# Chunk 0's x by selection matrices, sums of channels two heads at a time, and a new order of the first third of the tasks, in a kernel of a recurrence and an MLP

## The chip, the core and the metric

The kernel runs on one core of a Trainium2 chip. The metric is the device time of one execution in microseconds. A core has five engines that run their own instruction queues side by side and meet at semaphores: TensorE (PE) for matmuls, VectorE (DVE), ScalarE (ACT), GpSimd (POOL) and SyncE (SP), which here issues the DMA transfers. All data are in float32.

## What is computed

For each batch and head a state of 40 x 40 is carried over 768 steps, read by r and updated with w, a, b, k and v. The outputs y of the 8 heads of a token stand side by side as a row x of 320 values, which goes through an MLP with a quick GELU.

```python
batch, n_heads, seq, head_dim = (4, 8, 768, 40)
for t in range(S):
    y[:, :, t] = np.einsum('bhd,bhde->bhe', rt, state)
    Sa = np.einsum('bhde,bhe->bhd', state, at)
    state_decay = state * wt[:, :, None, :] - np.einsum('bhd,bhe->bhde', Sa, bt)
    state = state_decay + np.einsum('bhd,bhe->bhde', vt, kt)
x = np.ascontiguousarray(attn_out.transpose(0, 2, 1, 3)).reshape(B * S, H * D)
h = x @ w_in                                # 320 x 2048
g = h * (1.0 / (1.0 + np.exp(-1.702 * h)))
return (g @ w_out).astype(np.float32)       # 2048 x 320
```

## The kernel before

The sequence is cut in 12 chunks of 64 steps, and the four batches in two pairs. A chunk of one pair is a unit; there are 24, and unit i belongs to chunk i // 2. Inside a unit the recurrence is turned into matrix work on 64 x 64 blocks, in these steps (names are those of the tiles):

- `load_w`, `logarithm`, `decay`: the decays w are loaded (`logw`), their logarithm is taken on ScalarE, and they are summed over time on PE with the triangular matrix `edges`. `by_time` writes the sums of all channels side by side (`ps_cum`). For units 0 to 3 `by_channel` writes the same sums with the channels on partitions (`ps_cumc`), one head to each of the four 64 x 64 quarters of PE, 16 matmuls per unit; later units get those by two scans on VectorE from a second tile `wc`. Exponentials of the sums are FT, GT and G.
- `prep`: a, k, b and the tiles `kh`, `bh` are multiplied by FT, GT or G, and the scores A and RV are made.
- `inverse`: the product N of a and b goes through five levels of an iteration for a triangular inverse. For units 0 to 3 (`plain_level`) a level is 16 matmuls with EX and PT and four with `ident` into `ps_level`, a copy of PT on ScalarE (or VectorE), and a transpose to EX on VectorE. After the last level Q, Tc, QT and T21 complete T.
- `solve`: B, then X = T B on PE, M on VectorE, then `read` writes `ps_y`. Its left part is y, its right part the next state (`zraw`, `zr`, `zT`, `rz` in the next unit of the pair). `decayed` multiplies y by FT to x, which lies with 40 channels on each half of the partitions.
- `part_with` writes x to DRAM in two transfers and `get_back` reads it in two (one for each half of the partitions) as `xT_all`, with 64 partitions of five rows of 128 tokens, so that a matmul contracts 64 of the 320 channels. `w_in` is laid out on the host in the same order of channels (`order`).
- `mlp`: per chunk `up` (160 matmuls of 64 x 64 x 256, four at a time), GELU, and `down` (128 matmuls of 64 x 64 x 320). `weight` turns the MLP weights, which come as 64-bit numbers in eight pieces of four transfers, into float32: one step on ScalarE (`rebased`), three on VectorE (`bounded`, `shifted`, `rounded`) and one on GpSimd (`joined`) for each piece.

The order of all this is written out by hand: `ORDER` is a text of task numbers, each with a letter for the engine, and `listed` turns it into the program. A digit behind p, a, d or g names the pair of PSUM banks; behind s it is the number of transfers that may be under way before the next one starts. Tasks are numbered as `plan.add` is called; the costs given there were for the planner that made the text, and the kernel does not use them. All matmuls but the new ones go through `mm` (L301), all transfers through `transfer` (L331), so the profile shows those lines for them.

## Time and profile before

| | us |
|---|---|
| median of 3 runs | 681.54 (681.05 to 681.87) |
| the profiled execution | 679.49 |
| its span, first to last instruction | 677.7 |
| PE busy | 649.6 |
| VectorE busy | 449.7 |
| ScalarE busy | 329.1 |
| GpSimd busy | 175.7 |

In a row of a group, "out<-in" names the tiles, "x" the number of instructions; behind the bar stand the busy time in us and the mean of one in ns, then the idle time ahead of them and what ended it. In a row of the timeline stand the start, the length, the engine, the line and the tiles. A float32 matmul of the program is two MATMUL records in the trace, so the counts there are twice those of the code. TensorE's matmuls overlap: the start of the next group, not the end of the last matmul, tells how long a group held the engine.

### The profile page before, as it was taken

How to read it: one execution, taken by the hardware profiler on the slowest of the kernel's cores; microseconds unless marked ns; L12 is line 12 of the kernel's file. 1: busy time of each engine (PE TensorE's matmuls, PEld its weight loads, DVE VectorE, ACT ScalarE, POOL GpSimd, SP SyncE). 2: the span in 40 equal slices, each digit the busy share in tenths (PEclk: the TensorE clock that was granted, in tenths of full speed). 3: DMA queues.
4: the chain of work that ended last, by engine and by line, in shares of the span. 5: the costliest groups of instructions: out<-in, count | busy, mean ns of one | idle time of the engine just before them, and what ended most of it. 6: DMA issues, size and time to landing. Idle time of an engine off the chain costs nothing.

```text
span 677.7 us, 42447 instructions
## 1 busy us (share of the span) xinstructions
PE 649.6 (96%) x19616; PEld 568.7 (84%) x19616; DVE 449.7 (66%) x916; ACT 329.1 (49%) x681; POOL 175.7 (26%) x201
## 2 busy tenths in 40 slices
PE   5777999999999999999999999999999999999997
PEld 4667787787999997888888899999889798799896
DVE  5777779777867668757776687868656766675001
ACT  3676745634564655654545445455344454263010
POOL 6541443324123123123113211322411421300000
PEclk9979999999999999999999999999999999999999
DMA  6875753415324314432404513513412411200200
GB/s 208 295 255 160 226 172 97 129 42 152 107 64 131 94 58 124 114 107 65 124 14 131 149 35 108 155 33 107 140 38 62 130 53 45 69 15 14 60 13 21
DMA packets 35473, 69.74 MB, mean 103 GB/s; under 512 B 5472, under 2 KB 14816, under 8 KB 35296
## 3 DMA queue, kind: packets, MB, share of 16 engines
q1 hardware_dynamic: 35216, 66.99, 32.9%
q8 instruction: 154, 2.52, 1.6%
q14 instruction: 23, 0.19, 0.1%
q10 hardware_dynamic: 80, 0.04, 0.0%
HBM read 59.15 MB, written 7.86 MB: 99 GB/s over the span
## 4 chain that ended last, share of the span: by engine, by line
PE 88%; DMA 6%; DVE 2%; issue 1%; SPq 1%; ACT 1%; DVEq 0%; ACTq 0%
PE ps_up L301 31%; PE ps_down L301 29%; PE ps_level L301 8%; PE ps_y L301 5%; PE ps_B L301 4%; PE ps_X L301 2%; PE ps_N L301 2%; PE ps_rz L301 1%; PE ps_RV L301 1%; PE ps_A L301 1%; PE ps_zT L301 1%; SPq L331 1%; DMA w_sb<-in_w_in 1%; PE ps_cum L301 1%; PE ps_T L301 1%
## 5 line engine op out<-in xcount | busy, mean ns | idle before, releaser
L301 PE MATMUL ps_up<-xT_all,w_sb 64*64 64x256 f32 x3840 | 253.3, 377 | 2.1 <-issue 1.3
L301 PE MATMUL ps_down<-w_sb,g 64*64 64x320 f32 (+1 forms) x3200 | 241.5, 419 | 0.2 <-ACT zr L879 0.2
L301 PEld LDWEIGHTS ps_up<-xT_all,w_sb 64*64 64x64 f32 x3840 | 170.8, 133 | 18.8 <-issue 2.1
L301 PEld LDWEIGHTS ps_down<-w_sb,g 64*64 64x64 f32 x3200 | 142.5, 133 | 31.6 <-issue 0.4
L1000 ACT ACTIVATE g<-ps_up 128x1024 f32<-128x1024 f32 x48 | 49.2, 1025 | 46.3 <-PE ps_up L301 45.8
L719 POOL TENSOR_TENSOR EX<-ES,quads 128x512 f32<-128x512 f32 x30 | 39.7, 1324 | 116.4 <-DVE ES L712 77.7
L761 ACT COPY W<-ps_level 128x512 f32<-128x512 f32 x56 | 32.8, 585 | 67.7 <-PE ps_level L301 66.0
L301 PEld LDWEIGHTS ps_level<-W,EX 64*64 64x64 f32 x2560 | 60.0, 134 | 5.4 <-DVE T L840 0.2
L763 DVE TENSOR_TENSOR E<-two,ps_level 128x256 f32<-128x256 f32 x80 | 33.1, 415 | 36.5 <-ACT W L761 32.3
L301 PE MATMUL ps_level<-W,EX 64*64 64x64 f32 (+1 forms) x2560 | 56.8, 217 | 0.0
L717 ACT ACTIVATE EX<-ES,quads 128x256 f32<-128x256 f32 x82 | 37.2, 501 | 31.9 <-DVE ES L712 31.3
L629 POOL TENSOR_TENSOR ak<-ak,FT 128x512 f32<-128x512 f32 x17 | 23.0, 1353 | 77.2 <-DMA ak<-in_ak 54.4
L301 PEld LDWEIGHTS ps_level<-PT,EX 64*64 64x64 f32 x1280 | 30.7, 138 | 11.5 <-DVE EX L733 3.3
L301 PE MATMUL ps_level<-PT,EX 64*64 64x64 f32 (+2 forms) x1280 | 32.5, 234 | 6.9 <-DVE EX L733 5.0
L712 DVE STREAM_TRANSPOSE ES<-E 128x256 f32<-128x256 f32 x80 | 35.3, 443 | 4.4
L301 PE MATMUL ps_y<-RV,kh 64*64 64x104 f32 (+1 forms) x768 | 35.4, 247 | 0.9 <-DVE M L917 0.9
L301 PE MATMUL ps_y<-M,bh 64*64 64x104 f32 (+1 forms) x768 | 35.5, 247 | 0.7 <-DVE M L917 0.5
L901 ACT COPY B<-ps_B 128x416 f32<-128x416 f32 (+1 forms) x35 | 17.2, 493 | 34.4 <-PE ps_B L301 34.2
L301 PEld LDWEIGHTS ps_y<-RV,kh 64*64 64x64 f32 x768 | 29.6, 133 | 3.2 <-DVE M L917 1.5
L917 DVE TENSOR_TENSOR M<-ps_X,later 128x832 f32<-128x832 f32 (+1 forms) x24 | 23.9, 995 | 10.2 <-PE ps_X L301 10.0
L301 PE MATMUL ps_B<-RV,A 64*64 64x104 f32 (+1 forms) x768 | 29.2, 252 | 0.8 <-issue 0.8
L637 POOL TENSOR_TENSOR kh<-time,G 128x320 f32<-128x320 f32 x18 | 16.2, 901 | 51.2 <-PE ps_y L301 34.6
(133 smaller groups left out, 1099.0 us busy)
## 6 DMA issues: line engine op xcount, KB each, us to landing
ak<-in_ak SPq DMA_DIRECT2D x48, 160.0 KB
rv<-in_rv SPq DMA_DIRECT2D x48, 160.0 KB
time<-in_time SPq DMA_DIRECT2D x24, 320.0 KB
xT_all<-x_dram SPq DMA_DIRECT2D x48, 160.0 KB
wc<-in_wc SPq DMA_DIRECT2D x20, 264.0 KB
logw<-in_w SPq DMA_DIRECT2D x24, 160.0 KB
RV<-in_v SPq DMA_DIRECT2D x24, 160.0 KB
b<-in_b SPq DMA_DIRECT2D x48, 80.0 KB
```

What stands on the lines that cost most here:

```text
L301: nc.tensor.matmul(o, lhsT, rhs, start=start, stop=True, skip_group_check=True)
L331: begun.append(queue.dma_start(dst, src).ins)
L629: plan.add(R, {"DVE": 690.0, "POOL": 1270.0, "sbuf": True}, lambda t: of(t.engine).tensor_mul(ahT(), ahT(), FT_of(i)), reads=T("ak", "FT") ...
L637: plan.add(R + 4, {"POOL": 870.0, "DVE": 490.0, "sbuf": True}, lambda t, n=n, dst=dst: of(t.engine).tensor_mul(dst(i)[:, :, :D], by_head(t ...
L712: plan.add(rank, dve(256), lambda t: nc.vector.transpose(ES(n), source(t)), writes=[key("ES", n, 6)], **reads)
L717: nc.scalar.activation(dst[:, :, h], ES(n), ACT.Copy, scale=quads[:, h, :1])
L719: of(t.engine).tensor_mul(dst, ES(n).unsqueeze(2).to_broadcast([128, 8, 2, 32]), quads.unsqueeze(1).to_broadcast([128, 8, 2, 32]))
L761: plan.add(rank, any2(512), lambda t: copy(t.engine)(tiles_of(W(n + 1)), blocks(psum(t, ""), 64)), writes=[key("W", n + 1, 5)], pair=pair)
L763: plan.add(rank, dve(256), lambda t: nc.vector.tensor_sub(tiles_of(E(n + 1)), every(two32, [128, 2, 4, 32]), blocks(psum(t, ""), 64)[:, :, ...
L901: plan.add(R, any2(4 * wide), lambda t: copy(t.engine)(dst(), some(psum(t, "")[:, :, :208])), writes=[("Bv", i)] if x and c > 0 else T("B" ...
L917: plan.add(R + 1, dve(8 * wide), lambda t: nc.vector.tensor_tensor(M_of(i)[:, :, :wide].rearrange("p (j b) n -> p b j n", b=2), some(psum( ...
L1000: plan.add(-45, {"ACT": 1030.0, "table": "gelu"}, lambda t: nc.scalar.activation(g_of(c * NQ + q).rearrange("p m r n -> p r m n"), psum(t, ...
```

## The change

There are four parts.

1. Chunk 0 (units 0 and 1) no longer goes through DRAM. `first_x` multiplies y by FT in two VectorE instructions instead of four. `chosen` then moves the channels to their partitions with five matmuls per unit against selection matrices of zeros and ones, one with 512 columns and four with 128, and one copy brings the result from PSUM to `xT_all`. `selections` builds the two matrices once, in six instructions at the start.
2. The order of channels in x, and with it that of the rows of `w_in`, is another one. For chunks 1 to 11 `get_back` therefore reads each unit by four transfers: for each half of the partitions one of four rows and one of the fifth.
3. Units 0 to 3 load w as `in_apart`, with each head's 40 channels padded to 64 by ones, into the tile `wc` (256 KB instead of 160). `by_channel` then takes two heads in one matmul over 128 columns of weights, 8 matmuls per unit instead of 16. The padded columns of `logw`, and the three instructions that cleared them, are gone.
4. `ORDER` is new in its first third. On PE the two programs are the same from the 254th group of equal matmuls on, out of 953; in it and on the other engines the work of the first units stands in another order: the first load is w of unit 0, then `time`, a and k, a quarter of a weight piece, and b; N of unit 0 stands ahead of A and RV; and the first `up` matmul stands behind level 4 of unit 2 and A of unit 3 in both, and behind RV of unit 3 in the old order alone.

```diff
-    logw_t = several("logw", [128, DM + 24])
-    for t in logw_t:
-        nc.gpsimd.memset(t[:, DM:], 0.0)
+    logw_t = several("logw", [128, DM])
...
-    logw_of = lambda i: logw_t[i % 3][:, :DM]
+    logw_of = lambda i: logw_t[i % 3] if i >= BY_PE else apart(i).rearrange("p (h d) -> p h d", h=H)[:, :, :D]
 
     wc_of = lambda i: buf("wc", i, [128, 2, 8 * 33])
+    apart = lambda i: wc_of(i).rearrange("p n h -> p (n h)")[:, :H * 64]
 
     def load_w(i):
-        for name, of, src, n in (("wc", wc_of, wc_d, 528), ("logw", logw_of, w_d, DM))[i < BY_PE:]:
+        for name, of, src, n in (("wc", wc_of, wc_d, 528), ("logw", logw_of, w_d, DM)) if i >= BY_PE else (("wc", apart, apart_d, H * 64),):
...
-            ps, lw = psum(t, "ps_cum"), logw_of(i)
+            ps, lw = psum(t, "ps_cum"), logw_of(i) if i < BY_PE else logw_of(i).rearrange("p (h d) -> p h d", h=H)
             for n in (1, 0):
                 for b in BITS:
                     u = b ^ n
-                    mm(ps[HALF[u], b, :160], incl[HALF[b]], lw[HALF[b], n * 160:(n + 1) * 160], True)
-        plan.add(R, pe((1, 160)), by_time, reads=T("log"), uses=T("logw"), room=T("G"), writes=T("cum"), pair=("cum", i))
+                    mm(ps[HALF[u], b, :160].rearrange("p (h d) -> p h d", d=D), incl[HALF[b]], lw[HALF[b], 4 * n:4 * n + 4], True)
+        plan.add(R, pe((1, 160)), by_time, reads=T("log"), uses=T("logw") if i >= BY_PE else T("wc"), room=T("G"), writes=T("cum"), pair=("cum", i))
 
         def by_channel(t):
 
             ps = psum(t, "ps_cumc")
             for u, f in product(BITS, BITS):
-                for b, e in QUARTERS:
-                    o, h = (2 * u + f) * 65, head(e, f, b, u) * D
-                    mm(ps[HALF[e], b, o:o + 65], logw_t[i % 3][HALF[b], h:h + 64], edges[HALF[b]], o == 0)
+                for b in BITS:
+                    o, h = (2 * u + f) * 65, head(0, f, b, u)
+                    mm(ps[:, b, o:o + 65], apart(i)[HALF[b], 64 * h:64 * h + 128], edges[HALF[b]], o == 0)
...
-                y = both(i)[:, at, :64] if c > 0 else part(t)[:, u, 2 * b:2 * b + 2, :64]
-                of(t.engine).tensor_mul(x[:, b ^ u, b], y, FT_of(i)[:, at])
-        if c > 0:
-            plan.add(R + 6, {"DVE": 1200.0, "POOL": 2300.0, "sbuf": True}, decayed, reads=T("y", "FT"), uses=T("rz"), writes=T("x"))
-        else:
-            plan.add(R + 6, {"DVE": 1000.0}, decayed, reads=T("FT"), writes=T("x"), pair=("y", i))
-
-
-        rows = lambda: drams[i].rearrange("(e d j) n -> e d (j n)", e=2, d=D)
+                of(t.engine).tensor_mul(x[:, b ^ u, b], both(i)[:, at, :64], FT_of(i)[:, at])
+
+        def first_x(t):
+
+            x = x_of().rearrange("p (u f) b t -> p b u f t", f=2)
+            y, FT = (v.rearrange("p u (b f) t -> p b u f t", f=2) for v in (part(t)[:, :, :, :64], FT_of(i).rearrange("p (u j) t -> p u j t", u=2)))
+            for b in BITS:
+                nc.vector.tensor_mul(x[:, b, ::1 - 2 * b], y[:, b], FT[:, b])
+
+        def chosen(t):
+
+            ps = psum(t, "ps_xT")
+            nc.tensor.matmul(ps[:, 0], first_sel, x_of().rearrange("p j b t -> p (j b t)"), start=True, stop=True, skip_group_check=True)
+            for j in range(4):
+                nc.tensor.matmul(ps[:, 1, :128], rest_sel[:, 3 - j:131 - j], x_of()[:, j].rearrange("p b t -> p (b t)"),
+                                 start=j == 0, stop=True, skip_group_check=True)
+
+        rows = lambda: drams[i].rearrange("(d e j) n -> e d (j n)", e=2, d=D)
 
         def part_with(t):
             if i not in drams:
...
 
         def get_back(t):
             for h in HALF:
-                transfer(t, xT_of(c)[h, p].rearrange("q k n -> q (k n)"), drams[i].rearrange("(q k) n -> q (k n)", q=64))
-        plan.add(-50, {"SP": 700.0}, part_with, reads=T("x"), writes=T("xd"), size=DM * 512)
-        plan.add(-50, {"SP": 700.0}, get_back, reads=T("xd") + ([("weight", raws.index("x"))] if c in (1, 2) else []), writes=[("xT", c), ("xs", (c, p))], size=2 * DM * 512)
+                transfer(t, xT_of(c)[h, p, :4].rearrange("q k n -> q (k n)"), drams[i][:256].rearrange("(q k) n -> q (k n)", k=4))
+                transfer(t, xT_of(c)[h, p, 4], drams[i][256:])
+        if c > 0:
+            plan.add(R + 6, {"DVE": 1200.0, "POOL": 2300.0, "sbuf": True}, decayed, reads=T("y", "FT"), uses=T("rz"), writes=T("x"))
+            plan.add(-50, {"SP": 700.0}, part_with, reads=T("x"), writes=T("xd"), size=DM * 512)
+            plan.add(-50, {"SP": 2200.0}, get_back, reads=T("xd") + ([("weight", raws.index("x"))] if c in (1, 2) else []),
+                     writes=[("xT", c), ("xs", (c, p))], size=2 * DM * 512)
+        else:
+            plan.add(R + 6, {"DVE": 800.0}, first_x, reads=T("FT"), writes=T("x"), pair=("y", i))
+            plan.add(R + 7, {"PE": 1740.0, "instr": 20}, chosen, reads=T("x") + [("sel", 0)], pair=("xp", i))
+            plan.add(R + 7, any2(640), lambda t: copy(t.engine)(
+                xT_of(c)[:, p].rearrange("q k n -> q (k n)"), psum(t, "").rearrange("p r n -> p (r n)")[:, :640]),
+                     writes=[("xT", c), ("xs", (c, p))], pair=("xp", i))
...
+    def selections(t):
+
+        of(t.engine).memset(first_sel, 0.0)
+        of(t.engine).memset(rest_sel, 0.0)
+        first = first_sel.rearrange("p (h d e) -> p h d e", h=2, e=2)
+        rest = rest_sel[:, 3:131].rearrange("p (h d e j) -> p h d e j", h=2, e=2, j=4)
+        for e in BITS:
+            for to, cols in (first[HALF[e], :, :, e], slice(0, 32)), (rest[HALF[e], :, :, e, 0], slice(32, D)):
+                of(t.engine).tensor_copy(to, ident[HALF[e], cols].unsqueeze(1).to_broadcast([64, 2, cols.stop - cols.start]))
+    plan.add(0, {"POOL": 1600.0, "DVE": 900.0}, selections, writes=[("sel", 0)])
...
-    order = [d + D * (e + 2 * j) for e in range(2) for d in range(D) for j in range(H // 2)]
+    order = [q // 2 + D * (q % 2 + 2 * k) if k < 4 else 32 + q // 8 + D * (q // 4 % 2 + 2 * (q % 4)) for q in range(64) for k in range(5)]
...
+    apart = np.ones((4, 128, H, 64), np.float32)
+    apart[..., :D] = by_time[:4].reshape(4, 128, H, D)
```

283 lines of the change are left out of this document (143 added, 140 removed).

## Prediction

> **What bounds the kernel now.** I read the page first, then the busy time by stage, then TensorE's and VectorE's instructions in order of time up to the first matmul of the MLP.
>
> ```profile
> span 677.7 us, 42447 instructions
> PE 649.6 (96%) x19616; PEld 568.7 (84%) x19616; DVE 449.7 (66%) x916; ACT 329.1 (49%) x681; POOL 175.7 (26%) x201
> ```
>
> TensorE (PE) is busy for 649.6 of 677.7 us, so 28.1 us are idle. The view by stages (start:end, length, then busy time of PE, weight loads, DVE, ACT and POOL, the granted clock, the DMA share and GB/s) says where:
>
> ```profile
> 0.00:12.00 12.00, 4.42 (x116) 3.92 (x119) 6.42 (x13) 4.51 (x14) 7.83 (x40) 1.00 0.62 188
> 12.00:18.00 6.00, 5.33 (x156) 4.85 (x154) 2.45 (x5) 2.98 (x11) 2.50 (x2) 1.00 0.86 275
> 18.00:35.00 17.00, 11.61 (x475) 9.52 (x464) 14.23 (x22) 11.57 (x27) 8.52 (x5) 1.00 0.88 296
> 35.00:41.40 6.40, 5.37 (x136) 4.89 (x136) 4.04 (x8) 5.11 (x12) 3.13 (x2) 0.50 0.92 303
> 41.40:52.00 10.60, 8.14 (x352) 7.08 (x352) 9.05 (x16) 7.52 (x23) 4.84 (x3) 0.98 0.70 210
> 52.00:66.48 14.48, 10.64 (x496) 9.87 (x497) 10.58 (x22) 8.43 (x18) 1.69 (x2) 1.00 0.50 142
> 66.48:110.00 43.52, 42.13 (x1140) 35.12 (x1134) 35.46 (x56) 26.35 (x51) 21.65 (x12) 1.00 0.60 186
> 110.00:677.70 567.70, 561.97 (x16800) 493.50 (x16792) 367.47 (x781) 262.60 (x530) 125.58 (x136) 1.00 0.28 82
> ```
>
> Up to 66.48 us the idle time of PE is 7.58 + 0.67 + 5.39 + 1.03 + 2.46 + 3.84 = 21.0 us; from there it is 7.1 us. 66.48 is when the first MLP matmul starts, which needs chunk 0's x:
>
> ```profile
> 14.91 1.56 PE L301 MATMUL ps_level<-PT,EX 64*64 64x96 f32 x32 [0.67 <-DVE EX L733]
> 30.83 0.64 PE L301 MATMUL ps_level<-PT,EX 64*64 64x32 f32 x29
> 64.82 0.67 PE L301 MATMUL ps_level<-PT,EX 64*64 64x32 f32 x32 [0.84 <-DVE EX L733]
> 66.02 0.65 PE L301 MATMUL ps_A<-ak 40*64 40x64 f32 x32
> 66.48 2.48 PE L301 MATMUL ps_up<-xT_all,w_sb 64*64 64x256 f32 x40
> ```
>
> Rows 1 and 2 are level 0 and level 4 of unit 0's inverse, row 3 level 4 of unit 2. Before 66.48 PE has only the recurrence of units 0 to 3, a chain of short matmuls and VectorE steps; behind it MLP matmuls fill every gap. So the time is, nearly, the moment of the first MLP matmul plus the matmul work then left, and I cost the change by how far it moves that moment.
>
> **The change, part by part.** *The round trip of x.* Before, unit 0 and 1's x go out to DRAM and come back:
>
> ```profile
> 54.86 1.72 SPq L331 DMA_DIRECT2D xT_all<-x_dram  x2
> 61.39 1.09 SPq L331 DMA_DIRECT2D xT_all<-x_dram  x2
> ```
>
> The last read is issued from 61.39, and x is in use at 66.48. But in PE's order the first up matmul also stands behind level 4 of unit 2 and the scores A (and RV) of unit 3, which end just there: the row of 66.48 shows no idle time. In the changed order it stands behind the same level and A, and only RV of unit 3 (16 matmuls of A's shape, 66.48 - 66.02 = 0.46 us) comes after it. So removing the transfers by itself gives nothing; what counts is when that part of the chain is done.
>
> *The added matmuls.* Per unit one of 512 columns and four of 128, over the whole array. No row shows such a shape. At the pace at which 256 columns go through (80 records of four quarters, 4.32 us, quoted with the last chunk below: 0.216 us a pass, two passes per matmul) it is 0.86 + 0.86 = 1.7 us; if each of the ten passes ran alone, 3 us. Below the pace of the quarters I see no reason to go. I take 1.75, for it is a stream, and 3.5 us for both units. They lie where PE idles 2.46 + 3.84 us before 66.48 and VectorE sets the pace, so they cost nothing there; without that cover they cost 3.5.
> The cum sums by channel, eight wide matmuls for sixteen, stand in the same stage: nothing, give or take 0.3 us. The selection matrices are six small VectorE instructions at 4.7 us, where it waits for its first load.
> The Trainium skill, "TensorEngine Tiling (Array Packing)", Tiling Modes, says that changing the tiling mode drains TensorE; every matmul of before is cut in 64 or 40 rows, so no row shows a change. By that rule six groups of wide matmuls, entered and left, would add twelve drains; at 0.19 us, by which the matmuls of A outlast the start of the next group (0.65 - 0.46), an estimate of 2.3 us if none falls into idle time, 681.8 us in all, and nothing if all do.
>
> *The first levels.* The changed load order puts unit 0's rv behind 2.6 MB instead of 1.1 MB. At 188 GB/s to 12 us and 275 after, 2.6 MB are moved at 13.3 us; at 296 throughout, near 10. RV stands before level 0 on PE, so level 0 starts between 12.4 and 16.4 us, as against 14.91. I take 14.6: a queue with larger transfers should move faster than 188. Unit 1's matmul N no longer stands behind late VectorE steps, which gains a further us on level 1; so level 4 of unit 0 starts 1.1 us sooner, at 29.7 (bounds 2.1 sooner, 1.5 later), and ends 0.73 later, at 30.5.
>
> *From there VectorE's queue decides.* M of units 0 and 1 now:
>
> ```profile
> 40.92 1.02 DVE L917 TENSOR_TENSOR M<-ps_X,later 128x832 f32<-128x832 f32 x1 [0.90 <-PE ps_X L301]
> 49.34 1.02 DVE L917 TENSOR_TENSOR M<-ps_X,later 128x832 f32<-128x832 f32 x1 [1.10 <-PE ps_X L301]
> ```
>
> VectorE's groups up to 66.48 (line, shape, count, then busy us and mean ns of one) price its new order:
>
> ```profile
> L733 DVE STREAM_TRANSPOSE EX<-ps_level 128x512 f32<-128x512 f32 x14 | 9.9, 709 | 7.8 <-ACT PT L794 7.7
> L461 DVE TENSOR_SCALAR w_sb<-w_sb 128x1280 f32<-128x1280 f32 x4 | 3.9, 975 | 0.0
> L465 DVE TENSOR_SCALAR w_sb<-w_sb 128x1280 int32<-128x1280 int32 x4 | 3.3, 818 | 0.0
> L631 DVE SCALAR_TENSOR_TENSOR b<-b,GT 128x512 f32<-128x512 f32 x4 | 3.0, 738 | 0.0
> L726 DVE TENSOR_TENSOR PT<-ps_N,within 128x512 f32<-128x512 f32 x4 | 2.8, 692 | 2.6 <-ACT P L702 2.0 <-PE ps_N L301 0.6
> L648 DVE TENSOR_TENSOR A<-ps_A,upper 128x512 f32<-128x512 f32 x3 | 2.0, 665 | 0.0
> L962 DVE TENSOR_TENSOR x<-ps_y,FT 128x128 f32<-128x128 f32 x8 | 1.7, 276 | 0.5 <-PE ps_y L301 0.5
> L469 DVE TENSOR_SCALAR w_sb<-w_sb 128x1280 int32<-128x1280 uint32 x2 | 1.6, 804 | 0.0
> L840 DVE SCALAR_TENSOR_TENSOR T<-ps_T,quads,T 128x256 f32<-128x256 f32 x2 | 1.0, 482 | 0.0
> L794 DVE COPY PT<-ps_level 128x768 f32<-128x768 f32 x1 | 0.9, 940 | 0.0
> L855 DVE TENSOR_TENSOR zr<-zraw,wz 128x320 f32<-128x320 f32 x2 | 0.9, 465 | 0.0
> L904 DVE TENSOR_TENSOR B<-ps_B,B 128x416 f32<-128x416 f32 x1 | 0.6, 554 | 0.0
> L807 DVE COPY Tc<-ps_level 32x64 f32<-32x64 f32 x2 | 0.4, 220 | 0.0
> ```
>
> In the changed order: from the end of level 4 to the end of unit 0's M, ten copies Tc (2.2), a transpose (0.71), b (0.74), T (0.48), M (1.02), and two short transposes, QT and wz (1.4, by the 0.465 row): 6.5, so M ends at 37.0 instead of 41.9.
> From there to the end of unit 1's M: three evictions of 512 (0.69), three transposes (0.71; one by another line), A (0.67), five short ones (0.5 on average), x (4 x 0.276 = 1.1), two weight steps (0.98, 0.80), b (0.74), M (1.02): 12.0, so 49.0 instead of 50.4.
> From there to the copy that opens level 4 of unit 2: bounded and two shifts of the weights (2.6), x (1.1), four transposes (2.8), RV (0.67), a rounding (0.80), two sums wc (1.4, by the 512 rows), four short ones (2.0), the copy (0.94): 12.3, so 61.3. Then level 4 and A on PE, 66.48 - 64.82 - 0.46 = 1.2: the first up at 62.5, 4.0 us sooner. This holds VectorE at work all the time. ACT, PE and the loads are ready for each step in this order by the same rows, or late by some tenths; I leave those against the tenths by which instructions start before the one ahead has ended.
>
> *The reads back.* For chunks 1 to 11 each unit's x is now read by four transfers instead of two, on SP. Chunks 7, 8 and 11 use it soonest:
>
> ```profile
> 432.44 1.12 SPq L331 DMA_DIRECT2D xT_all<-x_dram  x2
> 436.73 0.38 PE L301 MATMUL ps_up<-xT_all,w_sb 64*64 64x256 f32 x1
> ...
> 487.28 1.12 SPq L331 DMA_DIRECT2D xT_all<-x_dram  x2
> 490.83 0.37 PE L301 MATMUL ps_up<-xT_all,w_sb 64*64 64x256 f32 x1
> 491.79 3.03 PE L301 MATMUL ps_up<-xT_all,w_sb 64*64 64x256 f32 x51 [0.59 <-DMA xT_all<-x_dram]
> ...
> 632.85 1.19 SPq L331 DMA_DIRECT2D xT_all<-x_dram  x2
> 637.07 4.32 PE ps_up L301 x80
> ```
>
> Chunk 8 waits 0.59 us for the second half, 4.4 us after the issue began; chunks 7 and 11 have 4.3 and 4.2 us and no slack to speak of. An issue takes 0.56 us. The second half's large piece is now issued one place later (the small last pieces are first needed 1.7 us into the up matmuls): 0.5 us at three places, 1.5 us. Bounds: nothing, if smaller pieces land sooner, and 2.2 us at each place (two places more per unit and as much again in the queue), 6.3.
>
> *Sum:* -4.0 (first up) + 0.46 (RV of unit 3 left over) + 1.5 = -2.0. The profiled execution took 679.49 us, so 677.5 by it; the median of the three runs shown, 681.54, is 2.05 above it, and the forecast for the median is 679.5 us, with 677.5 to 681 as its own range.
>
> **The rivals.**
> *Loads early, reads hidden.* Level 0 at 12.4 carries 2.1 us to the first up, and the reads cost nothing: 679.5 - 2.1 - 1.5 = 675.9. For it: DMA stood at a share of 0.62 to 12 us. Against: rv is one of the last of the first loads.
> *The clock falls again.* From 35 to 41.4 us the granted clock was 0.50, after a stretch in which PE worked 11.61 of 17 us; the 5.37 us of matmuls there took 2.7 us too long, ahead of the M that waits for PE at 40.92. My chain has them at full clock. If it falls once: 682.2, no change. The Trainium skill, "TensorE: Matmul & The Clock Gate", HAM oscillation, has the clock fall after an idle window of about 3.4 us; here it fell behind a stretch with PE at work two thirds of the time, so the trace goes further than the rule, and by the rule alone the loss would not come back and 679.5 would stand.
> *VectorE's queue has holes: slower.* Place: VectorE between M of unit 0 and level 4 of unit 2. It carries 24.3 us there, with the weights' steps ahead of x and of the transposes; in 41.4 to 52 us it was busy 9.05 of 10.6, in 52 to 66.48 only 10.58 of 14.48. At 0.85 the stretch takes 28.6 us, the first up comes at 66.8 and the time is 683.8; at those two shares in turn, 686.1. It decides from 3.4 us of holes on (683). For it: those shares. Against: units 2 and 3 and the weights stand interleaved, so a late step seldom leaves nothing to do, and what held VectorE at 52 to 66 was mostly ACT's copies (7.7 us of idle before EX in its group), of which two now go to VectorE.
> *The four reads late by 2.2 us at each of the three places: slower.* 679.5 - 1.5 + 6.3 = 684.3.
>
> **How the numbers follow.** Forecast 0.38, loads early 0.17, clock 0.12, holes 0.23, reads 0.10. What counts as no change is 0.2%, 1.36 us, about what a measurement of this kernel can tell: 680.2 to 682.9. Faster: 0.28 of the forecast's 0.38, the 0.17 and 0.05 of milder cases of the others, 0.50. Same: 0.10 of the forecast and 0.07 of the clock's, 0.17. Slower: 0.33. The range takes in 675.5 (loads early) and 684.5 (both slower rivals at their milder price).
>
> **What would show it.** The first up near 62.5 and the later matmuls dense; M of units 0 and 1 ending at 37 and 49; level 0 of unit 0 at 14.6; the wide matmuls at 1.7 us a unit; waits for x at chunks 7, 8 and 11 of half a us more. Wrong would be a first up at 66 or later with gaps on VectorE, a granted clock of 0.50 behind 20 us, or many waits for x after 110 us.

## The result, and the profile after

The changed kernel is slower: 689.05 us, the median of 9 runs (685.70 to 697.36), against 681.95 us (679.09 to 686.15, 9 runs) for the kernel before on the same chip. The ratio is 1.0098, with a 95% interval of 1.0069 to 1.0127. The forecast was 679.5 us, the range 675.5 to 684.5: wrong in sign and out of the range. One of the 9 runs (697.36 us) and two of one experiment below were in a slower state, which the ratios leave out; a ratio is therefore not exactly the quotient of two medians, but up to 0.2% from it. The profiled execution took 688.85 us.

First the page's busy times (us, share of the span, instructions), then the view by stages, with the columns as in the prediction, cut at the first up matmul of this kernel:

```profile
span 687.1 us, 42382 instructions
PE 657.4 (96%) x19572; PEld 576.4 (84%) x19572; DVE 450.9 (66%) x921; ACT 328.1 (48%) x674; POOL 180.1 (26%) x201
...
18.00:35.00 17.00, 11.76 (x392) 10.24 (x388) 11.26 (x16) 7.04 (x16) 4.35 (x5) 0.91 0.83 241
35.00:41.40 6.40, 4.03 (x165) 3.23 (x161) 4.29 (x13) 3.65 (x10) 3.57 (x2) 0.96 0.79 243
41.40:52.00 10.60, 9.06 (x274) 7.73 (x265) 10.23 (x20) 7.15 (x22) 4.00 (x4) 1.00 0.70 215
52.00:71.31 19.31, 15.85 (x636) 14.21 (x638) 18.43 (x27) 13.18 (x24) 8.14 (x4) 0.96 0.54 158
71.31:110.00 38.69, 37.63 (x1059) 31.83 (x1056) 33.58 (x55) 24.12 (x46) 16.14 (x8) 0.98 0.55 167
```

PE is busy for 7.8 us more and idle for 29.7 us instead of 28.1. VectorE was at work for 10.23 of 10.6 us and 18.43 of 19.31 us in the two stages where the prediction feared holes. Next, PE in order of time (start, length, line, operation, tiles, count, and in brackets the idle time ahead and what ended it), at the landmarks of the prediction:

```profile
4.10 1.97 PE L301 MATMUL ps_cumc<-edges,wc 64*128 64x65 f32 x16 [4.10 <-ACT wc L536]
10.35 1.23 PE L301 MATMUL ps_N<-b,ak 40*64 40x64 f32 x32 [3.52 <-DVE b L631]
12.78 1.97 PE L301 MATMUL ps_cumc<-edges,wc 64*128 64x65 f32 x16
16.12 1.51 PE L301 MATMUL ps_level<-PT,EX 64*64 64x96 f32 x32
25.17 0.47 PE L301 MATMUL ps_level<-PT,EX 64*64 64x96 f32 x11 [1.27 <-issue]
30.53 0.81 PE L301 MATMUL ps_level<-PT,EX 64*64 64x96 f32 x28 [2.60 <-issue]
35.31 0.70 PE L301 MATMUL ps_level<-PT,EX 64*64 64x32 f32 x32
71.31 1.93 PE L301 MATMUL ps_up<-xT_all,w_sb 64*64 64x256 f32 x16
```

And VectorE and GpSimd in order of time, M of units 0 and 1, then the stretch ahead of unit 2's level 4:

```profile
43.27 1.02 DVE L917 TENSOR_TENSOR M<-ps_X,later 128x832 f32<-128x832 f32 x1
55.12 1.01 DVE L917 TENSOR_TENSOR M<-ps_X,later 128x832 f32<-128x832 f32 x1
62.23 0.70 DVE L543 TENSOR_TENSOR_SCAN wc<-starts,wc 128x264 f32<-128x264 f32 x1
62.40 3.30 POOL L472 TENSOR_TENSOR w_sb<-w_sb 128x1280 int32<-128x1280 int32 x1 [1.24 <-DVE w_sb L468]
62.85 3.42 DVE L544 TENSOR_TENSOR_SCAN wc<-starts,wc 128x264 f32<-128x264 f32 x1
68.31 0.91 DVE L794 COPY PT<-ps_level 128x768 f32<-128x768 f32 x1
```

The first up matmul is at 71.31 us, 8.8 later than the 62.5 of the forecast. The landmarks split this. Level 0 of unit 0 starts at 16.12 instead of 14.6: +1.5. From there to level 4 it takes 19.2 instead of 15.1 us: +4.1. In it lie two stalls of PE (1.27 + 2.60 us) that the view puts down to no engine and no load of data, a granted clock of 0.51 from 32 to 35 us, where the forecast had it full, and in that stretch the wide sums of unit 2 (31.84 to 33.55); together they are more than 4.1, so other steps came sooner. From level 4 to the end of M, 9.0 instead of 7.3: +1.7. From M to M, 11.8 instead of 12.0. From there to the end of the copy that opens unit 2's level 4, 13.1 instead of 12.3: +0.8, with one scan of 3.42 us where 0.7 was priced. From the copy to the up matmul, 2.1 instead of 1.2: +0.9, at a granted clock that fell once more, to 0.66 from 69 to 74 us.

The first up matmul is not all of it. The changed kernel's span is 9.4 us longer than that of the kernel before: 4.8 us lie ahead of the first up (71.31 for 66.48) and 4.6 behind it (615.8 us for 611.2), where the sum had only 0.46 + 1.5.

Where such a stall of PE ("issue" in the rows) comes from is in the DMA records of the traces, under the queue of instructions:

```profile
q8 instruction: 154, 2.52, 1.6%
```

That is 154 transfers of 16 KB, one for every 254 of PE's 2 x 19572 records. The two stalls end at 25.17 and 30.53 us, and transfers of this queue had ended at 23.73 and 29.15. In the twenty profiles of this study there are, by accident, 154 stalls of 0.2 us or more as well, and 146 of them end 1.2 to 1.75 us behind the end of such a transfer, which comes every 4 us; by chance about one in seven would. So PE waits there for its own instructions. What makes a transfer late enough to be waited for, no run shows.

One more reading bears on what follows. Four kernels below differ from the kernel before only in how x is moved, and their first up matmul lay at 68.9 to 71.5 us in one profile each, not at 66.48. The one that differs only from chunk 1 on had it at 71.45, 5.0 us later. PE's stalls of this kind ahead of 75 us add up to 2.2 us in the profile of the kernel before and to 3.0 to 5.5 us in these four, so 66.48 was an early one. A single profile places the front to some 5 us at best, so I read sizes from the runs and only places from the profiles. The mean granted clock of each run, taken from 1 and multiplied by the span, says how much full speed was lost; over the 266 runs of this study, each kernel around its own mean, a microsecond lost cost 0.42 us. The mean loss of the changed kernel (5.0 us) is that of the kernel before (4.5 to 6.2 us in five sets of runs on three chips), so by this estimate the clock is not the difference between the two.

### The profile page after: what moved, and what is told of

It is laid out like the page before. It is cut to its first block, busy times and chain, and to the rows that moved or that the text cites. A ratio compares the mean times of both kernels' runs of the same rounds, so it can differ in the third digit from the quotient of the medians.

```text
span 687.1 us, 42382 instructions
## 1 busy us (share of the span) xinstructions
PE 657.4 (96%) x19572; PEld 576.4 (84%) x19572; DVE 450.9 (66%) x921; ACT 328.1 (48%) x674; POOL 180.1 (26%) x201
## 4 chain that ended last, share of the span: by engine, by line
PE 87%; DVE 5%; DMA 3%; issue 2%; SPq 1%; ACT 1%; POOL 0%; DVEq 0%; POOLq 0%; ACTq 0%
PE ps_down L301 29%; PE ps_up L301 29%; PE ps_level L301 9%; PE ps_y L301 4%; PE ps_B L301 4%; PE ps_X L301 2%; PE ps_A L301 2%; PE ps_N L301 1%; PE ps_rz L301 1%; PE ps_RV L301 1%; PE ps_zT L301 1%; PE ps_cum L301 1%; SPq L331 1%; DMA extra<-in_w_in 1%; DVE EX L733 1%
## 5 line engine op out<-in xcount | busy, mean ns | idle before, releaser
L301 PEld LDWEIGHTS ps_up<-xT_all,w_sb 64*64 64x64 f32 x3840 | 177.3, 134 | 16.2 <-issue 4.0
L301 PEld LDWEIGHTS ps_down<-w_sb,g 64*64 64x64 f32 x3200 | 140.4, 133 | 33.8 <-ACT zr L879 0.4
L717 ACT ACTIVATE EX<-ES,quads 128x256 f32<-128x256 f32 x76 | 34.5, 501 | 27.2 <-DVE ES L712 26.7
L629 POOL TENSOR_TENSOR ak<-ak,FT 128x512 f32<-128x512 f32 x18 | 24.7, 1371 | 83.6 <-DMA ak<-in_ak 47.2
L1048 DVE TENSOR_TENSOR ob<-ob,ps_down 128x320 f32<-128x320 f32 (+1 forms) x25 | 11.8, 471 | 27.9 <-ACT ob L1046 27.5
L301 PEld LDWEIGHTS ps_B<-RV,A 64*64 64x64 f32 x768 | 26.2, 135 | 4.1 <-DVE M L917 0.5
```

The costliest lines, as they stand in the source:

```text
L301: nc.tensor.matmul(o, lhsT, rhs, start=start, stop=True, skip_group_check=True)
L629: plan.add(R, {"DVE": 690.0, "POOL": 1270.0, "sbuf": True}, lambda t: of(t.engine).tensor_mul(ahT(), ahT(), FT_of(i)), reads=T("ak", "FT") ...
L717: nc.scalar.activation(dst[:, :, h], ES(n), ACT.Copy, scale=quads[:, h, :1])
L1048: plan.add(-45, dve(wide), lambda t: nc.vector.tensor_add(ob(), ob(), psum(t, "")[:, 1, :wide]), reads=[("ob", serial + n)], writes=[("out ...
```

## The experiments

"Of before" means the ratio to the kernel before on the same chip, with its 95% interval. 0.1% is 0.68 us.

### Operations against order

First all new operations in the old order: `ORDER` of before with the numbers shifted by one, the tasks of chunk 0's x replaced, and the banks of unit 1's y and unit 2's zT exchanged to make room.

```diff
+190p2 140p0 ... 335a3 141a0        chosen and its copy, unit 0
+193d0 195p3 ... 336a1 196a3        the same, unit 1
-192p3 194d3 193d3   315p0 317a0 316d0
+192p0 194d0 193d0   315p3 317a3 316d3
```

> All new operations (wide sums by channel, x of chunk 0 by selection matrices, reads in four) in the order of the kernel before; x of units 0 and 1 is chosen behind unit 1's X and behind unit 3's N. In the changed kernel the first up matmul came at 71.31 us instead of 66.48 and the time was 689.05 us instead of 681.95. If the operations themselves cost it (the wide sums took 1.90, 1.90, 1.71 and 1.04 us in the changed kernel, the narrow ones 1.12, 0.87, 0.51 and 0.74), this kernel has the first up at 68 to 70 us and takes 684 to 687 us. If the order costs it, the first up stays at 65 to 67 us and the time at 680 to 683 us.

688.78 us, 1.0112 of before (1.0063 to 1.0161), over the 684 to 687 us expected. The operations by themselves cost as much as the whole change.

The other way round, the kernel before in the changed order, with `part_with` and `get_back` of chunk 0 put among SP's loads:

```diff
-140p0 141a0 ... 195p2 196a2
+139s ... 140s ... 194s ... 195s4
```

> The operations of the kernel before (narrow sums, x of chunk 0 through DRAM, reads in two) in the changed order; the writes and reads of chunk 0's x stand on SP's queue a few places behind the x that they carry. If the order costs the time (two sums of a unit to come, 0.70 and 3.42 us on VectorE at 62.2 to 66.3 us, stand ahead of unit 2's last levels), the first up comes at 68 to 71 us and the time is 685 to 689 us. If the operations cost it, the first up is at 66 to 68 us and the time 681 to 684 us.

704.25 us, 1.0353 (1.0306 to 1.0399), far over either expectation, and so no measure of the order. The view of what the DMA queue waited for up to 95 us shows why: SP, whose list of loads has x in it, stood behind x twice (us in total, times, longest).

```profile
SPq L329 <- DVE x L960: 25.1, 2, 15.3
```

The loads behind it came late, and the clock lost 18 us of full speed. The changed order needs an x that SP has no part in.

### The wide sums

The changed kernel with narrow sums:

```diff
-                for b in BITS:
-                    o, h = (2 * u + f) * 65, head(0, f, b, u)
-                    mm(ps[:, b, o:o + 65], apart(i)[HALF[b], 64 * h:64 * h + 128], edges[HALF[b]], o == 0)
+                for b, e in QUARTERS:
+                    o, h = (2 * u + f) * 65, head(e, f, b, u)
+                    mm(ps[HALF[e], b, o:o + 65], apart(i)[HALF[b], 64 * h:64 * h + 64], edges[HALF[b]], o == 0)
```

> The changed kernel with the sums by channel as sixteen matmuls of a head each again, from the same padded tile. If the wide shape costs what its rows show (6.55 us for four units against 3.24 before) and that stands on the path, the first up comes 2 to 3.3 us sooner than 71.31 and the time falls to 685.5 to 687 us. If it lies in idle time of TensorE, as the prediction had it, nothing changes beyond 0.5 us.

685.27 us, 1.0079 (1.0048 to 1.0110): some of it may have come back, but the first up matmul came no sooner in its profile (72.56 us).

And the kernel before with wide sums alone, from a `logw` padded to 64 columns a head:

```diff
-                for b, e in QUARTERS:
-                    o, h = (2 * u + f) * 65, head(e, f, b, u) * D
-                    mm(ps[HALF[e], b, o:o + 65], logw_t[i % 3][HALF[b], h:h + 64], edges[HALF[b]], o == 0)
+                for b in BITS:
+                    o, h = (2 * u + f) * 65, head(0, f, b, u)
+                    mm(ps[:, b, o:o + 65], logw_of(i)[HALF[b], 64 * h:64 * h + 128], edges[HALF[b]], o == 0)
```

> The kernel before with the sums by channel two heads per matmul alone (from a tile of 64 columns a head). The rows of the changed kernel give 6.55 us for the four units' wide sums, the narrow ones took 3.24. If that lies on the path, the first up comes 2.5 to 3.5 us later than 66.48 and the time is 1.004 to 1.005 of before; if it is hidden, as predicted, the time is within 0.1% of before. If the wide shape in itself upsets the matmuls around it (a drain at each change of tiles), it is over 1.005.

683.93 us, 1.0058 (1.0036 to 1.0081): 3.9 us, between 2.4 and 5.5, for an edit that I had costed at nothing. The groups of PE up to the first up matmul, with their weight loads (PEld; count, busy us, mean ns, then the idle time ahead), first of the kernel before, then of this one:

```profile
L301 PE MATMUL ps_cumc<-edges,logw 64*64 64x65 f32 x128 | 3.6, 267 | 0.1
L301 PEld LDWEIGHTS ps_cumc<-edges,logw 64*64 64x64 f32 x128 | 3.3, 180 | 0.4 <-DVE A L648 0.4
```

```profile
L301 PE MATMUL ps_cumc<-edges,logw 64*128 64x65 f32 x64 | 6.2, 350 | 0.1
L301 PEld LDWEIGHTS ps_cumc<-edges,logw 64*128 64x128 f32 x64 | 5.5, 256 | 1.0 <-issue 0.4 <-DVE A L647 0.4
```

Half as many matmuls take 2.6 us more (in the changed kernel, where unit 2's ran at half clock too, 6.8 us with a mean of 378 ns: 3.2 more). In each of these kernels units 0 and 1 run at the slow pace: 16 wide records last 1.97 us there and 1.11 us for unit 3. The clock of 1.00 that the view by stages gives for this stretch rests on no record: the first clock record of a trace stands at 17.9 us (before), 18.4 (changed) and 21.1 us (this one). Fewer of them run side by side: 128 records of 267 ns in 3.6 us are 9.5 at a time, 64 of 350 ns in 6.2 us are 3.6. The Trainium skill, "TensorEngine Tiling (Array Packing)", Tiling Modes, which I had weighed for a drain at each change of mode (2.3 us for all wide groups), also lists two tiles for 64 x 128 and four for 64 x 64. The trace agrees with the second in its direction. But half as many matmuls, half as many at a time, would take as long as before; what is left is that each takes longer, its weight load with it (256 ns for 180). Why, these runs don't separate, nor whether a drain is in it.

The matmuls are not all of the 3.9 us either. The padded `logw` makes the loads of w larger (256 KB instead of 160), and they stand ahead of ak and rv on SP's queue. Unit 0's start, of the kernel before and of this one:

```profile
6.97 0.69 DVE L634 TENSOR_TENSOR ak<-ak,GT 128x512 f32<-128x512 f32 x1 [2.28 <-DMA ak<-in_ak]
8.91 1.02 PE L301 MATMUL ps_RV<-rv 40*64 40x64 f32 x27 [0.59 <-DMA rv<-in_rv]
```

```profile
9.25 0.69 DVE L633 TENSOR_TENSOR ak<-ak,GT 128x512 f32<-128x512 f32 x1 [4.56 <-DMA ak<-in_ak]
10.92 1.02 PE L301 MATMUL ps_RV<-rv 40*64 40x64 f32 x27 [0.63 <-DMA rv<-in_rv]
17.27 1.50 PE L301 MATMUL ps_level<-PT,EX 64*64 64x96 f32 x32
```

Level 0 is 2.4 us later (17.27 for 14.91), and 2.0 of these are there already when rv lands; unit 0's wide sums end inside the wait for it. The other kernels in the old order have this row of RV at 8.3 to 8.8 us with the small w and at 8.95 to 9.7 with the padded one, so the padding may be a part of the 2.0. No run pads w alone. Pairs in which both have the padded w and only the shape differs put the wide sums at 0.39% (1.0112 against 1.0073), 0.19% (1.0098, 1.0079) and 0.40% (1.0092, 1.0052, below): 1.3 to 2.7 us, with an interval that takes in zero in each.

### The scans beside GpSimd

```diff
-341d ... 271d                 VectorE's sums for units 5 and 4
+355d2 ... 341d 271d 49d       behind unit 3's RV, ahead of a shift of the weights
```

> The changed kernel with VectorE's sums for units 4 and 5 (two scans each) moved behind unit 3's RV, ahead of a shift of the fourth weight's parts, where GpSimd joins nothing. If these scans hold up unit 2's last levels (one of the two took 3.42 us beside GpSimd's join of weight parts, 0.70 us without), the first up comes some 3.5 to 4 us sooner, at 67 to 68 us, both long scans are back at 0.7 us and the time falls by 3 to 5 us, to 684 to 686 us. If VectorE is not what level 4 of unit 2 waits for, the first up stays within 1 us of 71.31 us.

688.63 us, 1.0092 (1.0055 to 1.0130): no change that can be told, and a first up at 70.97 us. The scans themselves became short, as expected; all four, in order of time, with GpSimd's next join:

```profile
74.58 0.70 DVE L541 TENSOR_TENSOR_SCAN wc<-starts,wc 128x264 f32<-128x264 f32 x1
75.19 0.68 DVE L542 TENSOR_TENSOR_SCAN wc<-starts,wc 128x264 f32<-128x264 f32 x1
75.79 0.68 DVE L541 TENSOR_TENSOR_SCAN wc<-starts,wc 128x264 f32<-128x264 f32 x1
76.39 0.68 DVE L542 TENSOR_TENSOR_SCAN wc<-starts,wc 128x264 f32<-128x264 f32 x1
...
77.88 2.98 POOL L470 TENSOR_TENSOR w_sb<-w_sb,extra 128x1280 int32<-128x1280 int32 x1 [11.99 <-DMA extra<-in_w_out]
```

Both edits together, narrow sums and the scans behind, were run twice:

> The changed kernel with both the narrow sums by channel (1.0079 of before by itself) and VectorE's sums for units 4 and 5 behind unit 3's RV (1.0092 by itself). If the two gains add up (the changed kernel stood at 1.0098), 1.006 to 1.008; if the long scan was what held up unit 2's levels and only the wide sums hid it, the first up comes at 66 to 68 us and the time is 1.000 to 1.004 of before.

683.34 us, 1.0052 (1.0033 to 1.0072). And on another chip, with twins that are told further down:

> The twin: the same with x written by two and read by four transfers (1.0052 of before, with 5.4 us of full speed lost on average). The same again, 1.003 to 1.007.

683.17 us, 1.0043 (1.0020 to 1.0065). Half of the loss is gone; it was the fastest version in the changed order, and still slower than the kernel before.

### What holds unit 1 in the changed order

The profile of its first run (narrow sums, scans behind) suggests why the order brings so little. Lines are two lower than in the changed kernel. ScalarE, VectorE, GpSimd and PE in order of time, from M of unit 0 to M of unit 1:

```profile
39.06 1.02 DVE L915 TENSOR_TENSOR M<-ps_X,later 128x832 f32<-128x832 f32 x1
45.14 0.48 DVE L838 SCALAR_TENSOR_TENSOR T<-ps_T,quads,T 128x256 f32<-128x256 f32 x1
46.55 1.37 ACT L454 ACTIVATE w_sb<-w_sb 128x1280 f32<-128x1280 f32 x1 [3.58 <-DMA w_sb<-in_w_in]
47.96 0.83 DVE L458 TENSOR_SCALAR w_sb<-w_sb 128x1280 f32<-128x1280 f32 x1 [2.34 <-ACT w_sb L454]
48.60 1.31 POOL L627 TENSOR_TENSOR ak<-ak,FT 128x512 f32<-128x512 f32 x1 [3.81 <-issue]
48.70 1.90 DVE L466 TENSOR_SCALAR w_sb<-w_sb 128x1280 int32<-128x1280 uint32 x1
49.88 1.86 POOL L632 TENSOR_TENSOR ak<-ak,GT 128x512 f32<-128x512 f32 x1
50.52 1.76 DVE L629 SCALAR_TENSOR_TENSOR b<-b,GT 128x512 f32<-128x512 f32 x1
52.96 1.56 PE L299 MATMUL ps_level<-PT,EX 64*64 64x96 f32 x32 [2.94 <-DVE EX L731]
57.26 1.03 DVE L915 TENSOR_TENSOR M<-ps_X,later 128x832 f32<-128x832 f32 x1 [0.67 <-PE ps_X L299]
```

The narrow sums bring M of unit 0 from 43.3 to 39.1 us. But a weight step stands in VectorE's queue ahead of b and of the next transpose; it waits 2.34 us for ScalarE's weight step, which waits 3.58 us for the weights to land, at 46.55 us. So the four microseconds are lost there and in what follows: from M to M it takes 18.2 us instead of 11.8. Behind it a weight step that took 0.82 us in the changed kernel (at 49.55 us), and the product b, which took 0.65 us for another unit in this one (at 37.81), take 1.90 and 1.76 us beside GpSimd's products, PE starves, and the clock falls, as the stages of the same kernel show:

```profile
48.80:52.30 3.50, 0.84 (x34) 0.56 (x32) 3.50 (x3) 3.34 (x9) 3.50 (x3) 0.87 0.71 202
52.30:58.30 6.00, 4.76 (x136) 4.61 (x136) 3.64 (x6) 1.31 (x3) 0.05 (x1) 0.50 0.35 101
```

In the ten profiles of the changed order taken here, the one with x on SP's queue aside, that step of ScalarE starts at 45.9 to 49.2 us, whether M of unit 0 starts at 37.75 or at 43.58. No run moves this step or its load, so that they hold unit 1 is read from the profiles and not tested.

The same kernel with fewer transfers of data under way, for PE's stalls (`s5` to `s8` made `s4` at 34 places):

```diff
-10s8 ... 6s3 ... 19s6 ... 53s8
+10s4 ... 6s3 ... 19s4 ... 53s4
```

> The changed order with narrow sums and the scans behind unit 3's RV (1.0052 of before), and nowhere more than 4 transfers under way where 5, 6 or 8 were allowed (34 places). If it is the bulk loads that keep TensorE's instructions waiting (stalls that nothing explains, 0.26 to 2.6 us each, 3.6 to 5 us ahead of the first up), they shrink to some 2 us as in the kernel before, and the ratio falls to 1.001 to 1.003. If the loads come too late instead, waits for rv, b or the weights appear and the ratio rises over 1.007.

686.10 us, 1.0087 (1.0057 to 1.0117): the loads came too late (ScalarE's step at 48.13 us after a wait of 5.08 us), and the stalls stayed: 0.2 to 1.35 us each ahead of 75 us, 3.8 us in all for 3.7. A miss: holding back the loads of data does not bring the instructions sooner.

### The selection matmuls

The new operations in the old order, as in the first experiment, but with narrow sums; the selection matmuls, the reads and the padded w are what is left of the change:

> The new operations in the old order (1.0112 of the time before) without the wide sums: sixteen matmuls of a head each, so that the selection matrices and the reads are what is left of the change. If the selection matmuls cost what they last (2.0 to 2.2 us a unit, two units) because TensorE's time ahead of the first up matmul isn't free, the first up is at 68 to 69 us and the time 1.005 to 1.007 of before. If they are hidden in idle time, as predicted, it is 0.999 to 1.002 of before, and the first up is at 65.5 to 67 us.

685.65 us, 1.0073 (1.0049 to 1.0097). Then the same with the five matmuls made twice:

```diff
+            for _ in BITS:
                 nc.tensor.matmul(ps[:, 0], first_sel, ...)
                 for j in range(4):
                     nc.tensor.matmul(ps[:, 1, :128], rest_sel[:, 3 - j:131 - j], ...)
```

> The new operations in the old order, narrow sums (1.0073 of before), with the selection matmuls of units 0 and 1 made twice: 2 x 2.1 us of TensorE more ahead of the first up matmul. If TensorE's idle time hides them, as the prediction said, the ratio stays at 1.007 (within 0.15%); if they stand on the path that sets the end, it rises by 4.2 us to 1.013 or 1.014; in between, the share of them that is on the path can be read off.

689.00 us, 1.0132 (1.0091 to 1.0174): 0.59% or 4.0 us more, with 0.1 to 1.1% by the two intervals. (The first set and the padded w, less the round trip that is saved, cost 0.24%, with an interval that takes in zero: 1.0073 against 1.0049 for the reads alone, below.) Unit 0's in order of time:

```profile
50.14 1.12 PE L972 MATMUL ps_xT<-x,first_sel 128*128 128x512 f32 x2
51.10 1.05 PE L974 MATMUL ps_xT<-x,rest_sel 128*128 128x128 f32 x8
51.99 1.02 PE L972 MATMUL ps_xT<-x,first_sel 128*128 128x512 f32 x2
52.85 1.05 PE L974 MATMUL ps_xT<-x,rest_sel 128*128 128x128 f32 x8
53.84 0.52 PE L299 MATMUL ps_zT<-ident,zr 40*40 40x40 f32 x32
```

A set lasts 1.9 us and PE goes straight on to zT, and behind unit 1's sets as straight to a level, so in the old order little hides it. And in the changed order, on top of narrow sums and the scans behind:

> The changed order with narrow sums and the scans behind unit 3's RV (1.0052 of before), with the selection matmuls made twice: 4.2 us of TensorE more. In the old order the second 4.2 us cost 4.0 us (1.0132 against 1.0073). If the changed order hides them in the idle time that VectorE leaves, as the prediction said, the ratio stays within 0.15% of 1.005; if they stand on the path here too, it goes to 1.011.

686.40 us, 1.0069 (1.0042 to 1.0097), against 1.0052 and 1.0043 for one set: about 0.2%, between -0.1 and 0.5%. By the middle of it some 1.5 of the set's 3.7 us show there, so more than half is hidden, as predicted; the interval leaves room for all or hardly any, and the difference to the old order is not clear of noise.

### The four reads

The kernel before with the new order of rows and four reads per unit everywhere:

```diff
-                transfer(t, xT_of(c)[h, p].rearrange("q k n -> q (k n)"), drams[i].rearrange("(q k) n -> q (k n)", q=64))
+                transfer(t, xT_of(c)[h, p, :4].rearrange("q k n -> q (k n)"), drams[i][:256].rearrange("(q k) n -> q (k n)", k=4))
+                transfer(t, xT_of(c)[h, p, 4], drams[i][256:])
```

> The kernel before with part of the change alone: the rows of x and of the first weight in the new order, each unit's x read back by four transfers instead of two (for chunk 0 too). The changed kernel took 1.0098 of the time before, the new operations in the old order 1.0112. If the reads cost what the prediction said (0.5 us at three places; in chunk 0 up to 1 us more, for x comes back there too), the time is 682.5 to 684.5 us, 1.002 to 1.005 of before, with more idle time ahead of the first up matmul of chunks 7, 8 and 11. If the transfers are hidden, as the changed kernel's waits for x (0.3 us against 0.6) suggest, it is within 1.5 us of before.

682.80 us, 1.0049 (1.0033 to 1.0066). Then the rows as they were, and the reads cut for chunks 1 to 11 alone, or for chunk 0 alone:

```diff
+                if c > 0:                  # or c == 0
+                    transfer(t, xT_of(c)[h, p, :4], rows_q[:, :4])
+                    transfer(t, xT_of(c)[h, p, 4], rows_q[:, 4])
```

> The kernel before, rows of x as they were, with each read of x for chunks 1 to 11 cut into two (four of a block, one of a block), chunk 0 read in two. The kernel before with four reads everywhere and the new order of rows took 1.0049 of before; behind its first up matmul it was not longer (609.8 us against 611.2). If the reads of the later chunks cost it, this one is at 1.003 to 1.005. If it was chunk 0, this one is within 0.1% of before.

> The kernel before, rows of x as they were, with only chunk 0's reads of x cut into two each (1.59 us of issuing more for two units: 2.45 + 2.87 us against 1.72 + 1.09, with loads behind them on SP's queue). If these are what the four reads cost (1.0049), this one is at 1.003 to 1.005, and the changed kernel, which has no reads in chunk 0, doesn't pay it. If the later chunks' reads cost it, within 0.1% of before. If neither of the two is slower, it is the new order of rows.

684.76 us, 1.0057 (1.0032 to 1.0081), and 679.72 us, 0.9987 (0.9959 to 1.0015). In the old order it is the later chunks. (The 1.59 us of the second expectation are 2.51 by the figures beside them; the result stands either way.) Then four writes and two reads:

```diff
-                transfer(t, rows()[e], x_of()[64 * e:64 * e + D]...)
+                transfer(t, drams[i].rearrange("(d e k) n -> e d k n", e=2, k=5)[e, :, :4], x_of()[64 * e:64 * e + 32]...)
+                transfer(t, drams[i].rearrange("(d e j k) n -> e d j k n", e=2, j=4, k=5)[e, :, :, 4], x_of()[64 * e + 32:64 * e + D]...)
```

> The kernel before with the new order of rows, but x laid in DRAM so that each unit's x is written by four transfers and read by two. Four reads of the later chunks alone cost 1.0057, and no wait for x shows it. If it is the number of transfers on SP's queue that costs (six a unit in place of four), this is at 1.004 to 1.006 as well. If it is that the reads end later or their small pieces, it is within 0.15% of before.

681.69 us, 1.0010 (0.9992 to 1.0029): it is not the number of transfers. In the changed order, with narrow sums and the scans behind, the same edit:

> The changed order with narrow sums, the scans behind unit 3's RV (1.0052 of before) and x of the later chunks written by four transfers and read by two. If the reads are the cost, 0.999 to 1.001 of before; if the number of transfers is, 1.004 to 1.007. What is then left over 1.000 is the selection matmuls less what the order gains.

> The changed order with narrow sums, the scans behind, x written by four and read by two, once more beside its twin with four reads. If the two ways of moving x cost the same in the changed order, both come to the same ratio within 0.2%, at 1.005 to 1.008; if the four reads cost 0.57% here as they did in the old order, this one is at 1.000 to 1.002 and its twin at 1.005 to 1.007; the 1.011 of its six runs before was then due to the clock, which lost 8.2 us of full speed on average in them.

687.87 us, 1.0110 (1.0080 to 1.0140), and 689.06 us, 1.0106 (1.0076 to 1.0137), where its twins with four reads came to 1.0052 and 1.0043. And in the changed kernel itself:

> The changed kernel as it is (wide sums, scans where they were), with x of the later chunks written by four and read by two. If the four reads cost 0.57% of its 0.98%, this is at 1.003 to 1.006; if they cost nothing in the changed order, it stays at 1.008 to 1.011.

689.12 us, 1.0106 (1.0067 to 1.0145), no better than its 1.0098. So what gained 0.5% in the old order loses 0.6% in the changed one with narrow sums, and these runs don't say why. The clock may be a part: the two kernels with two reads lost 8.2 and 6.9 us of full speed in the mean, their twins 5.4 and 5.6, which at 0.42 us each is an estimate of 0.5 to 1.2 us out of some 4. One profile has a second part, PE's waits for x (us in total, times, longest) in the repeat with two reads; its twin has none, and neither has the first run with two reads:

```profile
PE ps_up L299 <- DMA xT_all<-x_dram: 3.0, 4, 1.3
```

What the runs show is that four writes and two reads in place of two writes and four reads don't help the changed order. Whether two of each would, no run shows.

## Why the prediction was wrong

**"The cum sums by channel, eight wide matmuls for sixteen ...: nothing, give or take 0.3 us."** This step failed first. The rows of the wide sums are 2.6 to 3.2 us longer; by the runs they cost 1.3 to 2.7 us where the shape alone differs, each with an interval that takes in zero, and 3.9 us (2.4 to 5.5) together with the larger load of w in the old order. I had counted the matmuls: half as many, half as many at a time, is no gain, and each takes longer. Nor do they all lie in idle time. Unit 0's do: they end ahead of 3.52 us in which PE waits for b. But unit 1's (12.78 to 14.68 us) stand, with no idle time behind them, ahead of RV and level 0, which came 1.5 us later than forecast. M of unit 0 started at 41.5 to 43.6 us in the three profiles of the changed order with wide sums, at 37.75 to 40.8 in the seven with narrow ones.

**"From there VectorE's queue decides ... ACT, PE and the loads are ready for each step in this order by the same rows."** The second step that failed. The length from M to M was right in the changed kernel (11.8 for 12.0), but only because M of unit 0 was late. Where it came at 39.06 us, VectorE stood for a weight step whose load landed at 46.5, and M of unit 1 came at 57.26, not 12.0 us later at 51.1. M of unit 1 at 49.0 and the first up at 62.5 were out of reach in this order of loads, with wide or narrow sums. This is the rival of holes in VectorE's queue, at the place that it named, "with the weights' steps ahead of x and of the transposes"; I gave it 0.23 and argued against it that a late step seldom leaves nothing to do. In the changed kernel, with M of unit 0 some 4 us later, that wait was 0.47 us and VectorE was busy; I read this as the wide sums hiding the hole.

**"So the time is, nearly, the moment of the first MLP matmul plus the matmul work then left."** Single profiles don't bear this out. The kernel that reads chunk 0 by four had its first up 2.9 us later than the kernel before (69.37) and a span only 0.4 us longer (678.1); behind the first up the profiles took 608.6 to 616.0 us. And the 4.0 us were counted from 66.48, an early case.

**Prices taken from a mean.** Two sums were priced at 1.4 us and took 0.70 + 3.42; b at 0.74 took up to 1.76. All of them ran beside GpSimd. Moved away, the scan was back at 0.68 us, and that edit together with narrow sums brought 3.4 us or so (1.0098 to 1.0052 and 1.0043), though it brought nothing by itself.

**The selection matmuls** were sized right (1.75 forecast, 1.9 to 2.0 measured), and hidden mostly, as forecast: a second set cost 0.2% in the changed order and 0.6% in the old one, by the middle of wide intervals. That hiding may be all that the order gains: with narrow sums, 1.0079 in the changed order against 1.0073 in the old, and 1.0043 and 1.0052 with the scans behind. The -4.0 us of the sum was some -1.7 us at the best of these (0.25%), with an interval that takes in zero.

**The reads back**, 1.5 us: the waits that I forecast at chunks 7, 8 and 11 were not there (0.3 us of waiting for x in all, against 0.6 before). In the old order the four reads of the later chunks cost 3.9 us none the less (0.57%); in the changed order reading by two and writing by four saves nothing. Open. (Chunk 8's 4.4 us is 4.5 by its rows; no term changes.)

**The clock rival** was given 0.12. The clock did fall, to 0.51 from 32 to 35 and 0.66 from 69 to 74 us, but no more in the mean than before. The Trainium skill, "TensorE: Matmul & The Clock Gate", HAM oscillation, has the clock fall behind an idle window of about 3.4 us. This rule, which I had set against the trace, fares better than I gave it: in the kernel with narrow sums and the scans behind, PE had worked 0.84 of 3.5 us ahead of 52.3 us, from where the clock was 0.50. But where the clock fell at 32 us in the changed kernel, PE had been idle for 2.60 us in one piece at most.

None of these versions beat the kernel before by a measurable amount.

## What to carry to other kernels

Fewer matmuls are not less TensorE time: price a new shape from rows of that shape, weight loads included, or run it alone first, and where only a first-levels chain runs, take it to be on the path. When a chain is forecast to start sooner, look up for each step in its engines' queues when its load lands, above all for work of another stage (weights) that stands between its steps; the gain ends at the first load that doesn't move. Price VectorE steps that will meet GpSimd by the slowest row of their group, not by its mean.

## What the runs showed of the hardware that was not expected

- VectorE beside GpSimd: a scan of 264 columns took 3.42 us during a join of 3.30 us, 0.68 to 0.70 us otherwise, and ended 0.6 us after that join; b times GT took 1.76 us beside its products of ak for 0.65. Both read two operands from SBUF. A weight step with one took 1.90 us for 0.82 beside the same products. The Trainium skill, "GPSIMD Engine Reference", Specifications, says that GpSimd's SBUF interfaces are shared with VectorE, with contention for instructions with two SBUF inputs. The trace agrees; the size of it is what I had not expected.
- PE stalled for up to 2.9 us at a time for its own instructions, in every kernel here: 1.7 to 5.5 us in all ahead of 75 us, 0.5 to 5.1 us behind. Nearly all of these stalls (146 of 154) end 1.2 to 1.75 us behind the end of a 16 KB transfer of the queue of instructions. Fewer transfers of data under way did not cure it.
- Two ways to move the same x, behind the first up matmul, cost 0.5% one way in one order and 0.6% the other way in the other, with at most 1.1 us of waits for x in any profile but one (3.0 us). A gain of half a per cent measured in one order of tasks does not carry over to another.
